# Polysketch attention with a GELU layer on one core: chunk 0 alone first, and chunk 1 on the path of the later chunks

## The chip, the cores and the metric

The kernel runs on one core of one Trainium2 chip. Its time is the device time of one execution in microseconds (us): 259.19 us as the median of three runs (259.06 to 259.92). All matrices are float32. The two weight matrices and the two sketch matrices arrive as float64 and are turned into float32 on the chip.

## The reference

Attention with a product of two sketches as feature map, then an exact GELU layer. Batch 4, 4 heads, 1088 tokens, head size 32, sketch size 8; the layer goes from 128 to 2048 and back to 128.

```python
def phi(x):                                   # S1, S2: 8 x 32
    a = einsum('rd,bhsd->bhsr', S1, x)
    b = einsum('rd,bhsd->bhsr', S2, x)
    return einsum('bhsi,bhsj->bhsij', a, b).reshape(*x.shape[:-1], 64)
q_p, k_p = phi(q), phi(k)
kv  = einsum('bhsf,bhsd->bhfd', k_p, v)       # 64 x 32 for each head
z   = sum(k_p, axis=2)
num = einsum('bhsf,bhfd->bhsd', q_p, kv)
den = einsum('bhsf,bhf->bhs', q_p, z)[..., None] + 1e-6
x   = (num / den).transpose(0, 2, 1, 3).reshape(4352, 128)
h   = x @ w_in                                # 128 -> 2048
g   = 0.5 * h * (1 + erf(h / sqrt(2)))
out = g @ w_out                               # 2048 -> 128
```

## The kernel before

**Chunks and steps.** Each batch has 1088 tokens: two chunks of 512 and a rest of 64. Chunks are numbered n = 0 to 7 (two for each of the four batches), and the four rests together are chunk 8. For a chunk the 2048 hidden channels are taken in 16 slices of 128, called fi = 0 to 15. A step (n, fi) is: `hidden(n, fi)`, the 128x512 product of a slice of w_in with the chunk's attention output `xT[n]` (L721), followed by the GELU on ScalarE (L728). Below, h(n, fi) is that product and p(n, fi) the product of the GELU's result with the slice of w_out.

**Two ways to the output.** `project(n, fi)` (L858) is the plain way: one 128x512 product for each fi, added up in one PSUM bank. `two_products` (L807) is the other: four fi form a block, and seven pairs of half-size products take the place of the four plain ones (a Strassen-like scheme with 7 products in place of 8). It needs sums of the GELU's results, `token_sums` (L772 to L775, four GpSimd operations of 128x512 for a block), and sums of parts of w_out, `channel_sums(i)` (L759 to L762, four GpSimd operations for each piece of w_out). Before the change, chunks 0 and 1 use the plain way for fi 0 to 7 (`USUAL = 8`) and blocks for fi 8 to 15; later chunks use blocks from fi 0 (`first_block`).

**Two ways to the features of the queries.** Chunks 0 and 1 of the first batch use `query_turn` (for chunk 1 four TensorE transposes), `expand_products` with `expand_copy` and `expand_multiply`, then `numerators_by_token`, `divide` and a transpose back (`turn_half` for chunk 1). Later chunks use `query_turn` as one block transpose on VectorE (L528), `query_sketch(n)` (L578), `query_outer(n)`, a run of eleven VectorE lines from L590 to L613, and `attend(n)` (L633, copied to xT at L644). The second way needs the sums of the first batch in another layout: `spread_sketches` (eight GpSimd operations, L477 to L487), `repeat_first_z` (ScalarE copies and one GpSimd copy) and `turn_first_kv` (TensorE, then three small VectorE operations). For chunks 2 and later only batch 1 and above is needed at first, so here `turn_first_kv` comes late, in step 42.

**Rounding of the weights.** w_in and w_out come in five pieces each: pieces 0 and 1 hold two fi, pieces 2, 3 and 4 hold four fi. A piece lands as pairs of 32-bit words, and the class `Rounding` makes float32 of it: `low_words` (ScalarE L260), `fields` (VectorE L268 and L273), `exponents` (ScalarE L279), `mantissas` (VectorE L287, or, with `by_pool`, ScalarE L284 and then GpSimd L285), `signs` (VectorE L292) and `product` (L297, VectorE or GpSimd). h(n, fi) can start only when the piece of w_in is through, p(n, fi) only when that of w_out is.

**Order.** Every engine runs its instructions in the order of the program text (the last loop of the kernel adds this as a dependence). `at(t, f)` puts f into slot t; in step t the loop emits first `hidden`, then `token_sums` at the end of a block, then the slot's functions, then products of earlier steps. The steps of chunks 0 and 1 are interleaved by four fi:

```python
    steps = [(n, fi) for f in range(0, USUAL, 4) for n in range(NCH) for fi in range(f, f + 4)]
    steps += [(n, fi) for n in range(NCHUNK) for fi in range(USUAL if n < NCH else 0, NF)]
```

so that the order is chunk 0 fi 0 to 3, chunk 1 fi 0 to 3, chunk 0 fi 4 to 7, chunk 1 fi 4 to 7, then chunk 0 fi 8 to 15, chunk 1 fi 8 to 15, chunk 2 fi 0 to 15 and so on. Chunk 2 begins in step 32. Every load goes through SP's queue in the order of the text (k and q and v of the first batch, w_in pieces 0 and 1 with q of chunk 1 between them; then, behind a small GpSimd memset that waits for the rounding of w_in piece 0, w_out and w_in pieces 0 to 4, then the other batches).

Of the kernel before, what the change touches and what calls it, by code (L numbers as in the profile page):

```python
# [16 lines left out]
def kernel(  # L17
# [97 lines left out]
    def load_q(n):  # L115
        at = n % NCH * CW
        if n < NCH:
            sp.dma_start(out=q_sb[n], in_=q[0, :, at:at + CW, :].rearrange("h (p j) d -> p h j d", j=JC))  # L118
            return
        for h in range(H):  # L120
            sp.dma_start(out=q_sb[n][h * 32:(h + 1) * 32].rearrange("t x j d -> t (x j d)"),
                         in_=q[n // NCH, h, at:at + CW, :].rearrange("(t n) d -> t (n d)", t=32))
# [75 lines left out]
    load_w_in(0)  # L198
    load_q(1)
    load_w_in(1)  # L200

    def load_rest():

        load_w_out(1, gated=True)
        for i in range(2, len(pieces)):
            load_w_in(i)
            load_w_out(i)
        for b in range(1, B):
            load_keys(b)
            load_values(b)  # L210
            for c in range(NCH):
                load_q(b * NCH + c)
            if b == 1:
                for n, b1 in (("k", 1), ("k", 3), ("v", 1), ("v", 2), ("v", 3)):
                    load_rem(n, b1)
        load_q_rem()
# [26 lines left out]
    class Rounding:  # L243
# [37 lines left out]
        def mantissas(self, by_pool=False):  # L281
            if self.wide and by_pool:
                high = mlp.tile([128, LC // 2], FP, name="bits_high")[:, :self.m.shape[1]]
                act.activation(out=high, in_=self.a, func=ACT.Copy, scale=2.0 ** -20)  # L284
                pool.tensor_add(out=self.m, in0=high, in1=self.low)  # L285
            elif self.wide:
                dve.scalar_tensor_tensor(out=self.m, in0=self.a, scalar=2.0 ** -20, in1=self.low, op0=AX.mult,  # L287
                                         op1=AX.add)
# [209 lines left out]
    def repeat_first_z():  # L498
# [3 lines left out]
        for c in range(NP):  # L502
            act.copy(out=to[:F, c], in_=of[c * F:(c + 1) * F, :, 0:D])
        zs = att.tile([128, 2, D], FP, name="z_cols")
# [15 lines left out]
    def query_turn(n, copy=by_act):  # L520


        if n == 1:
            turned = transposed(work_bank(), "qT", [q_sb[1][:, h].rearrange("p j d -> p (j d)") for h in range(H)], copy)
            qT[n] = turned.rearrange("p (h j t) -> p h j t", h=H, j=JC)
            return
        qT[n] = att.tile([128, H, width[n] // 128, D], FP, name="qT" if n < NMAIN else "qT_rem")
# [184 lines left out]

    first_banks, begun = {}, [(0, 0), (1, 0)]

    def hidden(n, fi, by_halves=False):
# [3 lines left out]
        for rows in (slice(0, 64), slice(64, 128)) if by_halves else (slice(0, 128),):  # L719
            if (n, fi) not in begun:  # L720
                pe.matmul(ps[rows, :W], lhsT=w[:, rows], rhs=xT[n][:, :W], start=True, stop=True)  # L721
        if n < NCH and fi < USUAL:
            g_of[n, fi] = mlp.tile([128, CW], FP, name="g", bufs=4)
        else:
            if fi % NB == 0:
                blocks[n, fi // NB] = block(FP)
            g_of[n, fi] = blocks[n, fi // NB][:, fi % NB]
        act.activation(out=g_of[n, fi][:, :W], in_=ps[:, :W], func=ACT.Gelu)  # L728

    def first_hidden(n, half):  # L730

        if half == 0:
            first_banks[n, 0] = hidden_bank()
        parts = 1 if n else 2
        for i in range(parts):
            cols = slice(half * 256 + i * 256 // parts, half * 256 + (i + 1) * 256 // parts)
            pe.matmul(first_banks[n, 0][:, cols], lhsT=w_tile(w_in_sb, 0), rhs=xT[n][:, cols], start=True, stop=True)  # L737
# [53 lines left out]
    def first_block(n):  # L791
        return USUAL // NB if n < NCH else 0

# [53 lines left out]
    def project(n, fi, parts=range(B // 2), cols=slice(None)):  # L847
        first, final = fi == 0, fi == (USUAL if n < NCH else NF) - 1
        if first:
# [10 lines left out]
    def store(n):  # L860
# [9 lines left out]
        row = n // NCH * S + n % NCH * CW  # L870
        if n < NCH:

            for c in range(d_model // 32):
                to = out[row:row + CW, c * 32:(c + 1) * 32].rearrange("(g t j) d -> j t g d", t=32, j=JC)
                o = oT[c * 32:(c + 1) * 32].rearrange("p n (m d) -> p (n m) d", d=32)
                o = o.rearrange("p (g j) d -> j p g d" if n == 0 else "p (j g) d -> j p g d", j=JC)
                for j in range(JC):
# [48 lines left out]
    w_in[0].exponents()  # L926
    late = []
    query_turn(1, lambda **a: late.append(a))
    kz_of, kv_of = (x.rearrange("f (r x) -> f r x", r=2)[:, :, :C] for x in (kz[0], kv_bank[:, :128]))
    act.copy(out=kz_of, in_=kv_of)  # L930
    w_in[1].fields()
    w_in[0].mantissas()
# [4 lines left out]
    w_out = [Rounding(w, beside=b) for w, b in zip(w_out_sb[:2], w_in)]  # L937
    by_act(**late[0])
    w_in[1].low_words()
    parts = [range(2), range(2, JC)]  # L940
    nd = [[hidden_bank(), hidden_bank()], [out_bank(), out_bank()]]
# [3 lines left out]
    w_in[1].exponents()  # L945
    expand_products(1)
    for banks, tokens, by in zip(nd, parts, (None, den)):
# [3 lines left out]
    for half in range(2):  # L951
        first_hidden(0, half)
    expand_copy(1, 0)
    w_in[1].mantissas()
    w_in[1].signs()
    w_in[1].product()
    expand_copy(1, 1)
    for i in range(2):
        expand_multiply(1, i)
    w_out[0].fields()  # L960


    steps = [(n, fi) for f in range(0, USUAL, 4) for n in range(NCH) for fi in range(f, f + 4)]
    steps += [(n, fi) for n in range(NCHUNK) for fi in range(USUAL if n < NCH else 0, NF)]
    slots = {t: [] for t in range(len(steps) + LAG)}
# [83 lines left out]
    def kv_and_attend(b, n):  # L1049

        banks = held["kv"] = work_banks()
        kv_sum(b, banks[:, 1, CW // 2:])
        if n >= NCH:
            attend(n, banks)
        take_kv(b, banks[:, 1, CW // 2:])

    def round_at(t, w, product_by=dve):
        r = []
        at(t, lambda: (r.append(Rounding(w)), r[0].low_words(), r[0].fields()))
        at(t + 1, lambda: (r[0].exponents(), r[0].mantissas(), r[0].signs(), r[0].product(product_by)))  # L1060

    for i, (t0, t1) in enumerate(((4, 6), (8, 10))):
        round_at(t0, w_in_sb[i + 2])
        round_at(t1, w_out_sb[i + 2])
    round_at(12, w_in_sb[4], pool)
    at(13, channel_sums, 3)

    at(12, widen_v_rem, 1)
    for r in range(2):
        at(14, key_turn_blocks, 1, r)  # L1070
    round_at(14, w_out_sb[4], pool)
    at(15, query_turn, 2)
    at(16, features_of_all, 1)
    at(16, outer_of_all, 1)
    at(16, turn_keys_rem, 1)
    at(17, features_rem, 1)
    at(17, add_tokens, 1)
    at(18, channel_sums, 4)

    at(24, z_sum, 1)  # L1080
    at(24, fold_z, 1)
    at(23, query_turn, 3)
    at(24, kv_and_attend, 1, 1)
    at(24, query_sketch, 2)
    at(26, lambda: turn_kv(1, held["kv"]))
    at(24, query_outer, 2)
    for i, t in enumerate((25, 26, 28)):
        at(t, channel_sums, i)
    at(11, spread_sketches)
    at(40, repeat_first_z)  # L1090
    for n in range(3, NCHUNK):

# [32 lines left out]
        if keys:  # L1125
            at(t + 5 + (n == NCH + 1), outer_of_all, b)
            at(t + 5 + (n == NCH + 1), add_tokens, b)
            at(t + 8, widen_v_rem, b)
            if b == 2:
                at(t + 10, turn_first_kv)  # L1130

# [4 lines left out]
    for t, (n, fi) in enumerate(steps):  # L1136
        if n < NCH and fi < USUAL:
            products[t + LAG].append((project, n, fi))
            if fi == USUAL - 1:
                slots[t + LAG + 1 + 2 * n].append(lambda n=n: take_usual(n))  # L1140
        elif n == NMAIN:
# [8 lines left out]
        elif fi % NB == NB - 1:  # L1150
            b = fi // NB
            opens = b == first_block(n)
            late = int(n < NCH or n == NCH and opens)
            for later, pairs in ((3, 3), (4, 2), (5, 2)) if opens else ((2, 2), (3, 2), (4, 1), (5, 2)):
# [8 lines left out]
    for t in range(len(steps) + LAG):  # L1163
        if t < 4:
# [7 lines left out]
            if t == 2:  # L1172
                w_out[1].low_words()
            if t == 3:
                banks = work_banks()
                numerators_by_token(1, halves(banks), range(JC))
                w_out[1].mantissas(by_pool=True)
                w_out[1].exponents()
                divide(1, banks, range(JC), by_head_pair=False)
                w_out[1].signs()  # L1180
                w_out[1].product()
                project(0, 0)
                project(0, 1, cols=slice(0, 256))
                turn_half(1, 0, work_bank(), by_act)
                project(0, 1, cols=slice(256, 512))
                turn_half(1, 1, work_bank(), by_dve)
            continue
        if t == 4:
            first_hidden(1, 0)
            for f, *a in products[t]:  # L1190
                f(*a)
            first_hidden(1, 1)
        for n in drains[t]:
# [5 lines left out]
        if t < len(steps):  # L1199
            n, fi = steps[t]  # L1200
            hidden(n, fi, by_halves=t >= 18 and (n < NMAIN or fi < 5))
        if t < len(steps) and steps[t][0] < NMAIN and steps[t][1] % NB == NB - 1:
# [5 lines left out]
        for n in done[t]:  # L1208
            store(n)
        if t != 4 and not sooner:  # L1210
            for f, *a in products[t]:
# [42 lines left out]
```

## Time and profile before

| What | Value |
|---|---|
| median of three runs | 259.19 us (259.06 to 259.92) |
| span of the profiled execution | 257.9 us, so about 1.3 us of the median lie around it |
| PE busy | 253.1 us, 98% of the span |
| DVE, ACT, POOL busy | 151.1, 115.2, 163.6 us |
| granted TensorE clock | 0.999 of full |
| h(n, fi), one 128x512 product | 0.86 us from start to start |
| a block pair of `two_products` | 0.43 us |
| starts of h(0, 0), h(0, 8), h(2, 0) in the chain that ended last | 15.31, 45.70, 71.33 us |

PE is TensorE, DVE VectorE, ACT ScalarE, POOL GpSimd, SP the queue that issues loads and stores. In a line of the timeline the first number is the start in us, the second the duration in us, then engine, line of the kernel, operation, tiles and count; in square brackets is the idle time just before and what ended it. A float32 product is two PE instructions, so "x2" is one product. The displayed durations of PE run into each other by some 0.15 us, so that distances between starts are the price.

### The profile page before, as it was taken

The page shows a single profiled execution, that of the slowest core. Times are in us where ns is not written, and L with a number is a line of the kernel's source. Part 1 is how long each engine was busy: PE and PEld are TensorE (multiplying, and loading weights), DVE is VectorE, ACT ScalarE, POOL GpSimd, SP SyncE. Part 2 cuts the span into 40 slices and gives each one's busy share as a digit, 9 for nine tenths or more (in the row PEclk, how much of TensorE's full clock was granted, in tenths as well). Part 3 has the DMA queues.
Part 4 walks back from the last instruction along what each step waited for, and adds up shares of the span by engine and source line. Part 5 has one row for each costly group of instructions (what it writes and reads, how often), then busy time and mean ns, then how long its engine had stood idle before and what let it go on. Part 6 is the DMA issues. An engine that isn't in the chain of part 4 may idle for free.

```text
span 257.9 us, 5770 instructions
## 1 busy us (share of the span) xinstructions
PE 253.1 (98%) x2335; PEld 135.5 (53%) x2335; DVE 151.1 (59%) x313; ACT 115.2 (45%) x224; POOL 163.6 (63%) x173
## 2 busy tenths in 40 slices
PE   8989999999999999999999999999999999999995
PEld 7846444354444545444444455455544444445794
DVE  3786888969699997590178986399307000700330
ACT  4665777433626332543335332533444334433442
POOL 3313006799968778587758775787758777877300
PEclk9999999999999999999999999999999999999999
DMA  6459747751000101102000002000200200020020
GB/s 203 143 156 375 181 117 174 211 131 15 4 0 13 29 3 23 20 8 35 3 0 3 0 10 37 0 1 3 41 3 5 38 0 1 7 36 0 3 41 20
DMA packets 29594, 13.48 MB, mean 52 GB/s; under 512 B 21888, under 2 KB 27776, under 8 KB 29568
## 3 DMA queue, kind: packets, MB, share of 16 engines
q1 hardware_dynamic: 29392, 13.05, 20.2%
q8 instruction: 18, 0.29, 0.5%
q10 hardware_dynamic: 176, 0.07, 0.1%
q14 instruction: 8, 0.07, 0.1%
HBM read 10.88 MB, written 2.23 MB: 51 GB/s over the span
## 4 chain that ended last, share of the span: by engine, by line
PE 93%; SPq 2%; DMA 2%; DVE 1%; issue 0%; ACT 0%
PE h_ps L721 45%; PE o_ps L807 33%; PE o_ps L858 5%; PE w_ps L855 3%; DMA small<-in_moe_w_in_dram 2%; PE w_ps L437 1%; PE w_ps L578 1%; PE w_ps L633 1%; SPq L132 1%; PE h_ps L737 1%; SPq L100 1%; PE w_ps L977 1%; PE w_ps L656 0%; SPq L118 0%; PE w_ps L467 0%
## 5 line engine op out<-in xcount | busy, mean ns | idle before, releaser
L721 PE MATMUL h_ps<-xT,w_in 128*64 128x512 f32 (+3 forms) x514 | 136.9, 576 | 0.0
L728 ACT ACTIVATE block<-h_ps 128x512 f32<-128x512 f32 (+1 forms) x128 | 73.1, 571 | 117.2 <-PE h_ps L721 115.3
L721 PEld LDWEIGHTS h_ps<-xT,w_in 128*64 128x64 f32 (+1 forms) x514 | 41.9, 142 | 30.5 <-issue 11.6
L807 PE MATMUL o_ps<-block,w_out 128*64 128x256 f32 x224 | 57.5, 379 | 0.0
L772 POOL TENSOR_TENSOR bits_low<-block 128x512 f32<-128x512 f32 x28 | 36.0, 1286 | 27.7 <-ACT block L728 27.7
L807 PEld LDWEIGHTS o_ps<-block,w_out 128*64 128x64 f32 x224 | 30.5, 137 | 38.0 <-issue 27.5
L773 POOL TENSOR_TENSOR bits_a<-block 128x512 f32<-128x512 f32 x28 | 35.8, 1278 | 11.8 <-ACT block L728 11.8
L822 DVE COPY sums<-o_ps 64x256 f32<-64x256 f32 x8 | 3.3, 417 | 60.6 <-PE o_ps L807 60.6
L774 POOL TENSOR_TENSOR bits_e<-bits_a,block 128x512 f32<-128x512 f32 x28 | 36.1, 1288 | 2.2
L775 POOL TENSOR_TENSOR bits_m<-block,bits_e 128x512 f32<-128x512 f32 x28 | 35.9, 1282 | 2.2
L807 PE MATMUL o_ps<-bits_a,small 128*64 128x256 f32 x112 | 28.8, 379 | 0.0
L807 PE MATMUL o_ps<-bits_low,small 128*64 128x256 f32 x112 | 28.8, 379 | 0.0
L807 PE MATMUL o_ps<-block,small 128*64 128x256 f32 x112 | 28.8, 379 | 0.0
L807 PE MATMUL o_ps<-bits_m,w_out 128*64 128x256 f32 x112 | 28.7, 379 | 0.0
L807 PEld LDWEIGHTS o_ps<-block,small 128*64 128x64 f32 x112 | 15.2, 137 | 17.9 <-issue 10.8
L807 PE MATMUL o_ps<-bits_e,small 128*64 128x256 f32 x112 | 17.0, 383 | 0.0
L858 PE MATMUL o_ps<-g,w_out 128*128 128x512 f32 (+1 forms) x34 | 16.5, 572 | 0.0
L807 PEld LDWEIGHTS o_ps<-bits_m,w_out 128*64 128x64 f32 x112 | 15.3, 137 | 0.0
L807 PEld LDWEIGHTS o_ps<-bits_a,small 128*64 128x64 f32 x112 | 15.2, 137 | 0.0
L807 PEld LDWEIGHTS o_ps<-bits_low,small 128*64 128x64 f32 x112 | 15.2, 137 | 0.0
L590 DVE STREAM_TRANSPOSE w_ps<-w_ps 128x512 f32<-128x512 f32 (+1 forms) x7 | 4.8, 687 | 17.1 <-ACT xT L644 12.7
L807 PEld LDWEIGHTS o_ps<-bits_e,small 128*64 128x64 f32 x112 | 7.7, 137 | 10.6 <-issue 8.8
(195 smaller groups left out, 303.7 us busy)
## 6 DMA issues: line engine op xcount, KB each, us to landing
block<-in_moe_w_in_dram SPq DMA_DIRECT2D x3, 512.0 KB, 11.3
block<-in_moe_w_out_dram SPq DMA_DIRECT2D x3, 512.0 KB, 14.7
k<-in_k_dram SPq DMA_DIRECT2D x12, 128.0 KB, 2.9
v<-in_v_dram SPq DMA_DIRECT2D x12, 128.0 KB, 3.5
q<-in_q_dram SPq DMA_DIRECT2D x24, 64.0 KB, 2.1
out_dram<-oT SPq DMA_DIRECT2D x21, 64.0 KB, 2.2
k<-in_k_dram SPq DMA_DIRECT2D x2, 256.0 KB, 2.8
q<-in_q_dram SPq DMA_DIRECT2D x2, 256.0 KB, 3.9
```

Of the source, the lines that this page charges most:

```text
L100: eng.dma_start(out=main[n, b][:, heads], in_=src_of[n][b, heads, 0:MAIN, :].rearrange("h (p j) d -> p h j d", j=J))
L590: dve.transpose(out=tok, in_=ps[:, :, :H2])
L721: pe.matmul(ps[rows, :W], lhsT=w[:, rows], rhs=xT[n][:, :W], start=True, stop=True)
L728: act.activation(out=g_of[n, fi][:, :W], in_=ps[:, :W], func=ACT.Gelu)
L772: pool.tensor_sub(out=s[3], in0=a11, in1=a21)
L773: pool.tensor_add(out=s[1], in0=a21, in1=a22)
L774: pool.tensor_sub(out=s[2], in0=s[1], in1=a11)
L775: pool.tensor_sub(out=s[4], in0=a12, in1=s[2])
L807: pe.matmul(acc[n][bank][half * 64:(half + 1) * 64, col:col + HW], lhsT=fixed, rhs=moving, start=opens and e == 0 and name in "4715", stop ...
L822: dve.tensor_copy(out=N[lo, 0, one], in_=a0[lo, one])
L855: pe.matmul(o_of[n][i][:, :128], lhsT=g[:, i * 128:(i + 1) * 128], rhs=w_tile(w_out_sb, fi), start=first, stop=final)
L858: pe.matmul(o_of[n][:, cols], lhsT=w_tile(w_out_sb, fi), rhs=g[:, cols], start=first, stop=final)
```

## The change

Chunk 0 runs through its 16 fi in steps 0 to 15 and chunk 1 through its own in steps 16 to 31. Chunk 0 keeps the old ways; chunk 1 takes the later chunks' way, with `query_turn` on VectorE, `query_sketch(1)`, `query_outer(1)` and `attend(1)`, and with blocks from fi 0. The queries of chunk 1 are loaded after all weights, in the later chunks' layout. `spread_sketches`, `repeat_first_z` and `turn_first_kv` move to steps 4, 5 and 6 (before: 11, 40 and 42). The roundings move too: w_in piece 2 begins in step 2 and ends in step 3, w_out 2 is in step 4, w_in 3 in step 6, w_in 4 in step 8, w_out 3 in step 9, w_out 4 in step 14; in all of them GpSimd does the addition of the mantissas, and in all but w_in 2 the product as well. p(0, 0) to p(0, 3) all stand in step 3.

The diff, cut:

```diff
-        if n < NCH:
+        if n == 0:
             sp.dma_start(out=q_sb[n], in_=q[0, :, at:at + CW, :].rearrange("h (p j) d -> p h j d", j=JC))
...
     load_w_in(0)
-    load_q(1)
     load_w_in(1)
...
             load_w_in(i)
             load_w_out(i)
+        load_q(1)
...
-                high = mlp.tile([128, LC // 2], FP, name="bits_high")[:, :self.m.shape[1]]
+                high = mlp.tile([128, LC], FP, name="bits_high", bufs=1)[:, :self.m.shape[1]]
...
         for c in range(NP):
-            act.copy(out=to[:F, c], in_=of[c * F:(c + 1) * F, :, 0:D])
+            for to_rows in (slice(0, F), slice(F, 2 * F)):
+                act.copy(out=to[to_rows, c], in_=of[c * F:(c + 1) * F, :, 0:D])
...
-        if n < NCH and fi < USUAL:
+        if n == 0 and fi < USUAL:
             g_of[n, fi] = mlp.tile([128, CW], FP, name="g", bufs=4)
...
     def first_block(n):
-        return USUAL // NB if n < NCH else 0
+        return 0 if n else USUAL // NB
...
-    late = []
-    query_turn(1, lambda **a: late.append(a))
...
-    w_in[1].fields()
     w_in[0].mantissas()
...
-    by_act(**late[0])
     w_in[1].low_words()
+    w_in[1].fields()
...
-    expand_products(1)
...
-    expand_copy(1, 0)
...
-    expand_copy(1, 1)
-    for i in range(2):
-        expand_multiply(1, i)
     w_out[0].fields()
-    steps = [(n, fi) for f in range(0, USUAL, 4) for n in range(NCH) for fi in range(f, f + 4)]
-    steps += [(n, fi) for n in range(NCHUNK) for fi in range(USUAL if n < NCH else 0, NF)]
+    steps = [(n, fi) for n in range(NCHUNK) for fi in range(NF)]
...
-    for i, (t0, t1) in enumerate(((4, 6), (8, 10))):
-        round_at(t0, w_in_sb[i + 2])
-        round_at(t1, w_out_sb[i + 2])
-    round_at(12, w_in_sb[4], pool)
-    at(13, channel_sums, 3)
...
+    def round_begin(w):
+        r = Rounding(w)
+        r.low_words()
+        r.fields()
+        r.exponents()
+        return r
+
+    def round_end(r, product_by):
+        r.mantissas(by_pool=True)
+        r.signs()
+        r.product(product_by)
+
+    def round_at(t, w, product_by=pool):
+        at(t, lambda: round_end(round_begin(w), product_by))
+
+    round_at(4, w_out_sb[2])
+    at(4, spread_sketches)
+    at(5, repeat_first_z)
+    round_at(6, w_in_sb[3])
+    at(6, turn_first_kv)
+    at(6, query_turn, 1)
+    at(8, query_sketch, 1)
+    round_at(8, w_in_sb[4])
+    round_at(9, w_out_sb[3])
+    at(9, query_outer, 1)
+    at(10, channel_sums, 3)
     for r in range(2):
-        at(14, key_turn_blocks, 1, r)
-    round_at(14, w_out_sb[4], pool)
-    at(15, query_turn, 2)
-    at(16, features_of_all, 1)
+        at(13, key_turn_blocks, 1, r)
+    at(14, widen_v_rem, 1)
+    round_at(14, w_out_sb[4])
+    at(15, attend, 1)
+    at(15, features_of_all, 1)
...
-    at(18, channel_sums, 4)
...
-    for i, t in enumerate((25, 26, 28)):
+    at(16, channel_sums, 4)
+    for i, t in enumerate((17, 18, 19)):
         at(t, channel_sums, i)
-    at(11, spread_sketches)
-    at(40, repeat_first_z)
...
-            if b == 2:
-                at(t + 10, turn_first_kv)
...
-        if n < NCH and fi < USUAL:
-            products[t + LAG].append((project, n, fi))
+        if n == 0 and fi < USUAL:
+            products[t + LAG if fi >= 4 else 3].append((project, n, fi))
...
             if t == 2:
                 w_out[1].low_words()
-            if t == 3:
-                banks = work_banks()
-                numerators_by_token(1, halves(banks), range(JC))
+                w_out[1].exponents()
                 w_out[1].mantissas(by_pool=True)
-                w_out[1].exponents()
-                divide(1, banks, range(JC), by_head_pair=False)
                 w_out[1].signs()
                 w_out[1].product()
-                project(0, 0)
-                project(0, 1, cols=slice(0, 256))
-                turn_half(1, 0, work_bank(), by_act)
-                project(0, 1, cols=slice(256, 512))
-                turn_half(1, 1, work_bank(), by_dve)
+                third = round_begin(w_in_sb[2])
+            if t == 3:
+                round_end(third, dve)
+                for f, *a in products[t]:
+                    f(*a)
             continue
-        if t == 4:
-            first_hidden(1, 0)
-            for f, *a in products[t]:
-                f(*a)
-            first_hidden(1, 1)
...
-            hidden(n, fi, by_halves=t >= 18 and (n < NMAIN or fi < 5))
+            hidden(n, fi, by_halves=t >= 10 and (n < NMAIN or fi < 5))
```

## The prediction

> **What bounds the kernel now.** I read the page first: busy times, and the chain that ended last.
>
> ```profile
> PE 253.1 (98%) x2335; PEld 135.5 (53%) x2335; DVE 151.1 (59%) x313; ACT 115.2 (45%) x224; POOL 163.6 (63%) x173
> ...
> PE 93%; SPq 2%; DMA 2%; DVE 1%; issue 0%; ACT 0%
> ```
>
> TensorE sets the end and hardly stops. Then the timeline of PE, for what it does while the weights arrive.
>
> ```profile
> 0.77 3.22 PE L890 MATMUL w_ps<-const-float32-0.0 128*128 128x256 f32 x8 [0.77 <-PEq L1238]
> ...
> 29.23 1.02 PE L721 MATMUL h_ps<-xT,w_in 128*128 128x512 f32 x2
> 30.09 1.02 PE L858 MATMUL o_ps<-g,w_out 128*128 128x512 f32 x2
> 30.95 1.02 PE L721 MATMUL h_ps<-xT,w_in 128*128 128x512 f32 x2
> ...
> 45.53 1.02 PE L721 MATMUL h_ps<-xT,w_in 128*128 128x512 f32 x2
> ```
>
> From 24 to 43 us a hidden product and a plain projection alternate without a gap, 0.86 us each. h(0, 4) starts at 29.23 and h(0, 8) at 45.53: the two chunks share the work, so w_in 3 is wanted 16.3 us after w_in 2. Now VectorE, GpSimd, ScalarE and the loads, for how fast pieces can be rounded.
>
> ```profile
> 11.98 0.29 DVE L268 TENSOR_SCALAR bits_e<-small 128x256 uint32<-128x256 uint32 x1 [1.22 <-DMA small<-in_moe_w_in_dram]
> ...
> 13.07 0.22 DVE L673 TENSOR_SCALAR den_tok<-h_ps 128x4 f32<-128x4 f32 x2
> ...
> 27.35 0.69 DVE L297 TENSOR_TENSOR w_in<-bits_m,bits_e 128x512 f32<-128x512 f32 x1
> ...
> 33.97 0.69 DVE L297 TENSOR_TENSOR w_in<-bits_m,bits_e 128x512 f32<-128x512 f32 x1
> ```
>
> ```profile
> 22.47 0.58 POOL L487 COPY S_abc<-S_abc 128x64 f32<-128x64 f32 x3
> ...
> 40.89 1.28 POOL L297 TENSOR_TENSOR w_in<-bits_m,bits_e 128x512 f32<-128x512 f32 x1 [0.77 <-DVE bits_e L292]
> ...
> 49.37 1.28 POOL L772 TENSOR_TENSOR bits_low<-block 128x512 f32<-128x512 f32 x1 [1.15 <-ACT block L728]
> ```
>
> ```profile
> 24.84 0.66 ACT L260 ACTIVATE bits_low<-block 128x512 f32<-128x512 uint32 x1
> 25.40 0.59 ACT L728 ACTIVATE g<-h_ps 128x512 f32<-128x512 f32 x1
> 25.87 0.72 ACT L279 ACTIVATE bits_r<-bits_e,below 128x512 uint32<-128x512 uint32 x1
> ```
>
> ```profile
> 14.01 0.88 SPq L181 DMA_DIRECT2D small<-in_moe_w_out_dram  x2
> ...
> 18.53 4.49 SPq L106 DMA_DIRECT2D k<-in_k_dram  x4
> 25.46 7.04 SPq L113 DMA_DIRECT2D v<-in_v_dram  x4
> ```
>
> VectorE has w_in 3 ready at 34.66, eleven us early. GpSimd pays 1.28 us for a 128x512 operation where VectorE pays 0.69. The loads of v at 25.46 wait for the transfers of w_in 3 to w_out 4, the last by 32.1.
>
> **What goes from TensorE.** Four transposes of q (0.59, from 10.86 to 11.45), 16 products of `expand_products` (1.1), numerators (1.07), transposes back (0.44). Eight plain projections (8 x 0.86 = 6.88) become two blocks of seven pairs (14 x 0.43 = 6.02): 0.86 less. Added: sketch (0.60, 56.64 to 57.24) and attend (0.43), about 1.0. Behind the first hidden product this is 1.07 + 0.44 + 0.86 - 1.0 = 1.4 us less. `turn_first_kv` (0.3) only moves forward across step 32. The other removed products lie in the head, among waits.
>
> **The head.** VectorE no longer waits at 11.98 for w_in 1 before it rounds w_in 0; with 256 KB of q gone from the queue (about 1 us at the 269 GB/s of those slices) w_in 1 also lands near 11.0. den_tok moves from 13.07 to 11.95: all is 1.12 us earlier, so h(0, 0) starts at 15.31 - 1.12 = 14.19, and the gated loads at 12.35 for 14.01. Without the earlier landing it would be 0.67.
>
> **The price: the roundings.** Chunk 0 alone wants pieces twice as fast, and they now pass ScalarE, VectorE and GpSimd behind work that waits for TensorE. I lay the new order of each engine out by rows of before. ScalarE at 128x512: low words 0.66, exponents 0.71, GELU 0.60, the mantissa copy (seen at 128x256 only, 0.42) taken as 0.67; the next starts 0.1 before an end. VectorE: field 0.42, signs or product 0.69. GpSimd: 1.28 each. A handover costs 0.05.
>
> 1. h(0, 3) ends at 17.73. VectorE ends w_out 0 at 18.3 and w_out 1, with GpSimd's addition, at 20.65, and takes the fields of w_in 2 at 20.55 (landed by 22.8 before; 1.65 earlier now, at most 21.2). ScalarE: exponents to 21.73, then g(0, 3), mantissa copy to 22.8; GpSimd adds to 24.1; VectorE's product ends at 24.84. h(0, 4) starts at 24.9. Meanwhile TensorE has only p(0, 0) to p(0, 3), which wait for w_out 0 and 1 and for g(0, 3). Gaps: 0.6 + 0.6 + 0.7 + 1.8 = 3.7.
> 2. g(0, 4) ends at 26.4; behind it on ScalarE stands all of w_out 2 (26.3 to 28.14). GpSimd adds and multiplies to 30.8; behind this stand eight operations of `spread_sketches` (21.32 to 23.05 before, 1.7) and the z copy (about 0.3): 32.75. `turn_first_kv` stands on TensorE after h(0, 6), which ends at 27.5, and ahead of p(0, 4). Gap: 5.3.
> 3. GpSimd's w_in 3 ends at 35.3; h(0, 8) starts at 35.66 without a wait. g(0, 8) ends at 37.2, behind it w_in 4 on ScalarE to 38.94, GpSimd to 41.55; h(0, 12) at 41.75. Gap 0.45. h(0, 15) ends at 45.35.
> 4. w_out 3: VectorE's signs end at 41.35, and only then comes `query_outer(1)`, 57.40 to 63.7 before, 6.35 long: 47.7. `attend(1)` waits for it (gap 2.4); the features of batch 1's keys wait for VectorE's key transposes (49.05, gap 0.85). xT(1) stands on ScalarE behind w_out 4, whose fields VectorE takes at 49.0: 51.7. h(1, 0) starts at 51.75 after a gap of 0.85.
> 5. GpSimd: w_out 3 to 44.15, channel sums 3 (46.40 to 48.22 before) 1.85, token sums (0, 2) 5.2, v's rest 0.5, w_out 4 2.6, token sums (0, 3) 5.2, channel sums 4 1.85: 61.35. The first pair of block (0, 3) needs both, and TensorE arrives there at 56.4. Gap: 5.0.
>
> From there GpSimd (5.2 a block) keeps up with TensorE (4 x 0.86 + 3.01 = 6.45). From 61.4 to h(2, 0): 13 hidden products 11.2, 26 pairs 11.2, the batch's key sums and sketches 1.9 + 0.22 + 1.46: about 87.3, with two more pairs done than before (0.86) and `turn_first_kv` (0.3). Against 71.33 that is 87.3 - 71.33 - 1.16 = 14.8 us later. Check by gaps: 18.6 new, 1.3 of small ones in before's same stretch taken off, 1.4 of work and 1.12 of head off: 14.8. On the time this gives 259.2 + 14.8 = 274.0; the 1.3 around the span stay.
>
> **What a gap does to TensorE's clock.** The trace of before has no long gap but the one ahead of the first product; there 1664 columns of warming products took 3.22 us, which at the later 0.86 for 1024 columns take 1.40. So a gap costs between 0 and 1.8 us behind it. Two of mine exceed 5 us or come to it: 0 to 3.6. I take 1.8, one of two, since the nearest row is the start itself but its idle time is not that of a gap.
>
> The Trainium skill, "TensorE: Matmul & The Clock Gate", Part 1, says that the array falls to half its clock after an idle window of about 3.4 us, and comes back after about as long a busy one; the 656 ns of the first 128x256 products against 379 later agree with half a clock at the start, but no run here shows it in mid-kernel. By this rule each of the two gaps, longer than one window but shorter than two, may or may not hold a whole one; with both, an estimate from that page's 3.4 us is 1.7 us of loss each.
>
> Sum: 274.0 + 1.8 = 275.8.
>
> **What is hidden.** The queries of chunk 1 queue behind all weights, so land near 31; VectorE reaches them at 34.0. SP's later loads shift by four issues of 0.42; keys of batch 1 are wanted at 47.7. The doubled z copies, four of about 0.2 on ScalarE, are in step 2's chain beside GpSimd and cost nothing.
>
> **Bounds.** The channel sums at 42 to 45 took 0.64 to 0.91 instead of 0.46 beside busy VectorE: up to 1.6 more. Small gaps as before: 1.3. With both gaps cold, 274.0 + 3.6 + 1.6 + 1.3 = 280.5, and 1.2 if q lands as late as the slowest keys did (13.8 us after issue at 21.4): 282.
>
> **Rivals.** First: GpSimd's own work alone binds, the waits of step 2 to 4 vanish into it. From 22.85 its operations up to channel sums 4 are 1.28 + 10 x 1.28 + 1.7 + 0.3 + 1.85 + 5.2 + 0.5 + 5.2 + 1.85 = 30.6, ending at 53.45, 8 us earlier than 61.4: 266. For it: the scheme needs only ScalarE to run ahead; against it: ScalarE's roundings stand behind GELUs which wait for TensorE. Second: the loads last. If q_1 lands after 36, each us is one of delay at the sketch: 277 to 279. Against: the rows above give 31. Third, faster: the roundings stay ahead of TensorE, and the 1.4 of work, 0.3 of moved work and 1.1 of head remain: 259.2 - 2.8 = 256.4. It needs all gaps together under 2.8 us; step 1 alone has 3.7. That the change does not do what it says is excluded: the new order of instructions shows blocks of chunk 1 from fi 0.
>
> **Chances.** The chain 0.80 (274 to 282), GpSimd alone 0.12 (266), late loads 0.04, faster 0.04. Range 266 to 282, likeliest 275.8. A measurement of this kernel tells some 0.3% (0.8 us) from no change: faster 0.04, within 0.01, slower 0.95.
>
> **What would show it.** Right: PE gaps of about 5 us before L513 (released by POOL) and before the first L803 of block (0, 3) (by POOL), one before L630 (by DVE), h(2, 0) near 87 to 89. Wrong: no wait at L513, or h(0, 4) before 22, or gaps released by DMA.

## The result, and the profile after

The changed kernel takes 283.5 us (median of four runs, 282.21 to 284.49) against 259.36 us: 1.092 of before (95% interval 1.088 to 1.095), 24.1 us slower. The forecast of 275.8 had the sign and most of the mechanism, but the time lies 1.5 us above its range. The profiled execution took 284.49 us, its span 282.7.

The page after, for the two lines of before that were read first (busy time, and the chain that ended last by engine):

```profile
PE 259.4 (92%) x2315; PEld 134.3 (48%) x2315; DVE 152.6 (54%) x309; ACT 117.1 (41%) x228; POOL 184.7 (65%) x190
...
PE 77%; SPq 8%; POOL 6%; DMA 4%; DVE 2%; issue 1%; ACT 0%; POOLq 0%; DVEq 0%
```

TensorE's share fell from 98% to 92%: it is idle for 23.3 us of the span, 4.8 before. The chain's 8% of SPq and 4% of DMA come in at one GpSimd operation, the channel sum that starts at 51.48; GpSimd was at work until 51.51 (51.06 and 0.45), so the loads held up nothing there. The timeline of PE shows where; its brackets hold the gap and what ended it:

```profile
26.30 2.94 PE L718 MATMUL h_ps<-xT,w_in 128*128 128x512 f32 x6 [1.46 <-DVE w_in L297]
34.82 0.48 PE L513 MATMUL w_ps<-ident,z_cols 128*64 128x64 f32 x4 [5.59 <-POOL z_cols L506]
35.24 2.08 PE L854 MATMUL o_ps<-g,w_out 128*128 128x512 f32 x2
37.10 1.91 PE L718 MATMUL h_ps<-xT,w_in 128*128 128x512 f32 x2
38.81 1.92 PE L854 MATMUL o_ps<-g,w_out 128*128 128x512 f32 x2
40.52 1.27 PE L718 MATMUL h_ps<-xT,w_in 128*128 128x512 f32 x2
...
48.51 3.74 PE L718 MATMUL h_ps<-xT,w_in 128*64 128x512 f32 x16 [1.49 <-ACT block L725]
54.13 0.67 PE L630 MATMUL w_ps<-q_pT,kz_first 64*32 64x256 f32 x16 [1.89 <-DVE q_pT L610]
59.71 1.08 PE L718 MATMUL h_ps<-xT,w_in 128*64 128x512 f32 x4 [2.31 <-ACT xT L641]
68.37 0.69 PE L803 MATMUL o_ps<-block,small 128*64 128x256 f32 x1 [3.22 <-POOL small L758]
```

From the top: h(0, 4) to h(0, 6), then `turn_first_kv` behind 5.59 us of nothing, p(0, 4), h(0, 7), p(0, 5), h(0, 8), then h(0, 12), `attend(1)`, h(1, 0) and the first pair of block (0, 3). Four of these gaps are the forecast's, with the releasers it named. But the products behind the first one start 1.7 to 1.9 us apart instead of 0.86.

VectorE, where the lines L268 and L273 are `fields`:

```profile
12.56 0.83 DVE L273 TENSOR_SCALAR bits_a<-small 128x256 uint32<-128x256 uint32 x1
13.32 0.22 DVE L670 TENSOR_SCALAR den_tok<-h_ps 128x4 f32<-128x4 f32 x2
...
26.16 0.42 DVE L268 TENSOR_SCALAR bits_e<-block 128x512 uint32<-128x512 uint32 x1
...
29.86 1.50 DVE L268 TENSOR_SCALAR bits_e<-block 128x512 uint32<-128x512 uint32 x1
31.29 1.49 DVE L273 TENSOR_SCALAR bits_a<-block 128x512 uint32<-128x512 uint32 x1
...
36.78 0.83 DVE L268 TENSOR_SCALAR bits_e<-block 128x512 uint32<-128x512 uint32 x1
...
44.22 1.52 DVE L268 TENSOR_SCALAR bits_e<-block 128x512 uint32<-128x512 uint32 x1
45.66 1.50 DVE L273 TENSOR_SCALAR bits_a<-block 128x512 uint32<-128x512 uint32 x1
```

One form (128x512), two durations: 0.42 us, or 1.5, with one of 0.83 between. The timeline of GpSimd at the same moments:

```profile
12.52 0.73 POOL L297 TENSOR_TENSOR w_in<-bits_m,bits_e 128x256 f32<-128x256 f32 x1 [2.46 <-DVE bits_e L292]
...
29.82 1.26 POOL L285 TENSOR_TENSOR bits_m<-bits_high,bits_low 128x512 f32<-128x512 f32 x1 [4.30 <-ACT bits_high L284]
31.16 1.34 POOL L297 TENSOR_TENSOR w_out<-bits_m,bits_e 128x512 f32<-128x512 f32 x1
...
34.54 0.23 POOL L506 COPY z_cols<-kz 128x64 f32<-128x64 f32 x1
...
36.07 1.27 POOL L297 TENSOR_TENSOR w_in<-bits_m,bits_e 128x512 f32<-128x512 f32 x1
...
44.18 1.27 POOL L285 TENSOR_TENSOR bits_m<-bits_high,bits_low 128x512 f32<-128x512 f32 x1 [6.84 <-ACT bits_high L284]
45.53 1.34 POOL L297 TENSOR_TENSOR w_in<-bits_m,bits_e 128x512 f32<-128x512 f32 x1
```

Each 1.5 us field lies over a GpSimd addition or product and ends 0.28 or 0.29 us after it: 31.36 behind 31.08, 32.78 behind 32.50, 45.74 behind 45.45, 47.16 behind 46.87. The field at 36.78 began late in the product of 36.07, which ends at 37.34, and took 0.83. So a slowed field lasts as long as what is left of the GpSimd operation beside it, and then a little. (The 128x256 field at 12.56 lies in the same way over the product at 12.52.) GpSimd itself stands idle for 4.3 and 6.8 us until ScalarE has copied a mantissa, and ScalarE, in its own timeline, waits for those same fields with a GELU queued behind:

```profile
47.25 0.63 ACT L284 ACTIVATE bits_high<-bits_a 128x512 f32<-128x512 uint32 x1 [0.75 <-DVE bits_a L273]
47.78 0.58 ACT L725 ACTIVATE block<-h_ps 128x512 f32<-128x512 f32 x1
```

That GELU is what h(0, 12) at 48.51 waits for.

### The profile page after: what moved, and what is told of

It reads as the page before. It is cut to its first block, busy times and chain, and to the rows that moved or that the text cites. A ratio compares the mean times of both kernels' runs of the same rounds, so it can differ in the third digit from the quotient of the medians.

```text
span 282.7 us, 5739 instructions
## 1 busy us (share of the span) xinstructions
PE 259.4 (92%) x2315; PEld 134.3 (48%) x2315; DVE 152.6 (54%) x309; ACT 117.1 (41%) x228; POOL 184.7 (65%) x190
## 4 chain that ended last, share of the span: by engine, by line
PE 77%; SPq 8%; POOL 6%; DMA 4%; DVE 2%; issue 1%; ACT 0%; POOLq 0%; DVEq 0%
PE h_ps L718 36%; PE o_ps L803 32%; DMA block<-in_moe_w_out_dram 3%; PE w_ps L851 3%; SPq L121 2%; SPq L113 2%; SPq L106 1%; PE w_ps L437 1%; PE w_ps L886 1%; PE w_ps L575 1%; PE w_ps L630 1%; SPq L132 1%; DMA q<-in_q_dram 1%; POOL bits_m L771 1%; POOL bits_e L770 1%
## 5 line engine op out<-in xcount | busy, mean ns | idle before, releaser
L718 PE MATMUL h_ps<-xT,w_in 128*64 128x512 f32 (+3 forms) x532 | 139.7, 582 | 5.3 <-ACT xT L641 2.3
L725 ACT ACTIVATE block<-h_ps 128x512 f32<-128x512 f32 (+1 forms) x136 | 77.8, 572 | 130.3 <-PE h_ps L718 128.4
L803 PE MATMUL o_ps<-block,w_out 128*64 128x256 f32 x240 | 61.8, 380 | 0.0
L768 POOL TENSOR_TENSOR bits_low<-block 128x512 f32<-128x512 f32 x30 | 38.6, 1287 | 28.8 <-ACT block L725 28.8
L803 PEld LDWEIGHTS o_ps<-block,w_out 128*64 128x64 f32 x240 | 32.7, 137 | 40.6 <-issue 29.3
L769 POOL TENSOR_TENSOR bits_a<-block 128x512 f32<-128x512 f32 x30 | 38.2, 1272 | 16.0 <-ACT block L725 15.9
L771 POOL TENSOR_TENSOR bits_m<-block,bits_e 128x512 f32<-128x512 f32 x30 | 38.4, 1281 | 2.4
L803 PE MATMUL o_ps<-block,small 128*64 128x256 f32 x120 | 31.8, 388 | 3.2 <-POOL small L758 3.2
L803 PE MATMUL o_ps<-bits_low,small 128*64 128x256 f32 x120 | 31.8, 388 | 0.0
L285 POOL TENSOR_TENSOR bits_m<-bits_high,bits_low 128x512 f32<-128x512 f32 (+1 forms) x7 | 8.3, 1188 | 22.4 <-ACT bits_high L284 22.3
```

The source lines that it names most:

```text
L768: pool.tensor_sub(out=s[3], in0=a11, in1=a21)
L769: pool.tensor_add(out=s[1], in0=a21, in1=a22)
L771: pool.tensor_sub(out=s[4], in0=a12, in1=s[2])
L803: pe.matmul(acc[n][bank][half * 64:(half + 1) * 64, col:col + HW], lhsT=fixed, rhs=moving, start=opens and e == 0 and name in "4715", stop ...
```

## The experiments

Three theories stood at the start. The chain: the roundings pass three engines behind work that waits for TensorE. The clock: what the forecast left out is TensorE at half speed behind the gaps. The contention: what it left out is VectorE made slower by GpSimd. In all kernels but `e5_before_pool` the edit is made to the changed kernel. None leaves work out; `e1_warm`, `e7_dve_busy` and `e9_warm_all` add useless work.

**e1_warm: products of zeros in the longest gap.**

```diff
         ps, zs = work_bank(), held["zs"]
+        keep_busy(12, ps)        # 12 products 128x256 ahead of turn_first_kv
```

> The changed kernel (283.5 us) with twelve products of zeros, 128x256, on TensorE ahead of turn_first_kv, so 5.2 us of work without use in the gap of 5.6. Theory: the four 128x512 products behind that gap ran at 1.7 us instead of 0.86 because TensorE's clock fell in the gap; kept busy, the granted clock stays at 1.0 from 34 to 42 us, L513 still waits for the z copy to about 34.8, and the time falls by about 3.0 to 280.5. Rival: the slow products come from something else beside them (GpSimd and VectorE at work), then the time stays at 283.5.

Measured: 280.87 us, 1.082 [1.076, 1.087]; 2.6 less. The timeline of PE of this run:

```profile
25.67 4.54 PE L719 MATMUL h_ps<-xT,w_in 128*128 128x512 f32 x6 [1.46 <-DVE w_in L297]
30.05 5.39 PE L887 MATMUL w_ps<-const-float32-0.0 128*128 128x256 f32 x24
...
35.63 1.12 PE L855 MATMUL o_ps<-g,w_out 128*128 128x512 f32 x2
36.59 1.02 PE L719 MATMUL h_ps<-xT,w_in 128*128 128x512 f32 x2
```

The products behind the gap are back at 0.86 to 0.96 from start to start, at a granted clock of 1.00: the slow ones were the clock, not their data. (The z copy was through at 34.88, the zeros only at 35.4, so they held `turn_first_kv` back by some 0.5 us.) In this run h(0, 4) to h(0, 6) took 4.54 us instead of 2.94, at a granted clock of 0.58, with no gap over 1.5 us ahead.

**e2_early: the sketches spread before chunk 0.** `spread_sketches` and GpSimd's z copy move ahead of the steps, where GpSimd is idle.

```diff
     load_w_out(0, gated=True)
     load_rest()
+    spread_sketches()
+    repeat_first_z_cols()        # the GpSimd copy out of repeat_first_z
...
-    at(4, spread_sketches)
```

> The changed kernel with spread_sketches and the z copy on GpSimd put into its idle time after the memsets of the head (13 to 21 us), instead of behind the rounding of w_out 2. Theory (order on GpSimd): L513 does not wait any more; the next wait is p(0, 4) for w_out 2, ready at 32.5 where h(0, 6) ends at 29.2, so a gap of 3.3 in place of 5.6: 2.3 less, and up to 3.0 more if the clock holds through the shorter gap: 278 to 281. Rival (the gap is the roundings' alone): the wait only moves to p(0, 4) with its length, 283.5.

Measured: 281.3 us, 1.083 [1.079, 1.088]; 2.2 less, just above the expected 278 to 281. `turn_first_kv` starts at 30.09 without a wait, and the timeline of PE shows what is late next:

```profile
30.09 0.34 PE L516 MATMUL w_ps<-ident,z_cols 128*64 128x64 f32 x4
32.78 2.08 PE L857 MATMUL o_ps<-g,w_out 128*128 128x512 f32 x2 [2.35 <-POOL w_out L297]
```

p(0, 4) now waits for GpSimd's product of w_out 2, and runs at half clock as before. This run too has half clock at h(0, 4) to h(0, 6) (0.61 from 26 to 30 us).

**e3_dve: all roundings from w_in 2 on put on VectorE, all else as changed.** (Before the change GpSimd had the products of w_in 4 and w_out 4; here they are on VectorE as well.)

```diff
-        r.mantissas(by_pool=True)
+        r.mantissas()
...
-    def round_at(t, w, product_by=pool):
+    def round_at(t, w, product_by=dve):
```

> The changed kernel with the additions and products of w_in 2 to w_out 4 on VectorE as before the change (0.69 each instead of 1.28 on GpSimd). Theory: h(0, 4) comes 1.5 us earlier (no handover to GpSimd), w_out 2 is through by 30, spread and z copy run while GpSimd is idle, so the 5.6 gap falls to at most 1.6 and with it the cold clock; VectorE's fields at 128x512 take 0.42 again instead of 1.50, the query part starts earlier, and channel and token sums have no roundings ahead of them: 265 to 270. Rival (the engine does not matter, chunk 0 alone simply wants weights too early): 279 or more.

Measured: 270.96 us, 1.045 [1.043, 1.047]: 12.5 us less, somewhat short of the expected drop. The fields are at 0.42 us again, and `turn_first_kv` follows h(0, 6) at once. PE's list of waits (total, times, longest) shows what is left of the straight order:

```profile
PE w_ps L630 <- DVE q_pT L610: 3.2, 1, 3.2
PE o_ps L854 <- DVE w_out L297: 2.2, 3, 1.2
...
PE o_ps L803 <- POOL small L758: 0.6, 1, 0.6
```

VectorE now does all the rounding, and TensorE reaches `attend(1)` ahead of the end of `query_outer`: it waits 3.2 us, and behind it the granted clock is 0.58 for 4 us.

**e5_before_pool: only the other part, in the kernel before.** The old interleaved order, with GpSimd's addition and product in every `round_at`. (The tile of the copied mantissas is made as wide as in the changed kernel.)

```diff
-    def round_at(t, w, product_by=dve):
+    def round_at(t, w, product_by=pool):
...
-r[0].exponents(), r[0].mantissas(), r[0].signs()
+r[0].exponents(), r[0].mantissas(by_pool=True), r[0].signs()
```

> The kernel before the change (259.3 us), its steps interleaved as they were, but all roundings of w_in 2 to w_out 4 with addition and product on GpSimd as in the changed kernel. Theory: interleaved steps leave w_in 3 eleven us of slack, and each rounding gets only 1.2 us longer, so 259 to 261 us. Rival: GpSimd's roundings by themselves cost the time whatever the order of steps: 270 or more.

Measured: 262.7 us, 1.013 [1.011, 1.015]: more than the expected 259 to 261, far from the rival's 270. Its waits of PE:

```profile
PE o_ps L807 <- POOL bits_e L774: 1.5, 1, 1.5
...
PE h_ps L721 <- POOL w_in L297: 0.5, 1, 0.5
```

The swap of engines costs 3.2 us here and 12.5 in the straight order. The slow fields are here as well (L268 at 27.20 takes 1.51 us, L273 at 28.63 takes 1.49), so it is the order that decides how much of them is seen. Where a piece is wanted every 16 us, a slower rounding is nearly covered; where it is wanted every 8, it is not.

**e6_sooner: w_out 2 rounded a step earlier.**

```diff
             if t == 3:
+                fourth = round_begin(w_out_sb[2])
                 round_end(third, dve)
+                round_end(fourth, pool)
...
-    round_at(4, w_out_sb[2])
```

> The changed kernel (283.5 us) with the rounding of w_out 2 put from step 4 into step 3, so that on ScalarE its three operations stand ahead of g(0, 4), which waits for h(0, 4), and on VectorE its fields ahead of the product of w_in 2. Nothing else is moved, GpSimd does the same work. Theory (the gap at L513 comes from ScalarE's order): GpSimd's addition for w_out 2 starts at 26.2 instead of 29.8, the z copy ends near 31 instead of 34.8, the gap falls from 5.6 to about 2, and less clock is lost: 276 to 280. Rival (GpSimd's throughput sets the pace from here on, so it waits later for what it gains now): 282 or more.

Measured: 280.91 us, 1.083 [1.079, 1.088]; 2.6 less, between the expected 276 to 280 and the rival's 282. From its waits of PE:

```profile
PE h_ps L718 <- DVE w_in L297: 2.7, 1, 2.7
PE h_ps L718 <- ACT xT L641: 2.3, 1, 2.3
PE h_ps L718 <- POOL w_in L297: 2.3, 1, 2.3
...
PE w_ps L513 <- POOL z_cols L506: 0.5, 1, 0.5
```

The 5.6 us gap is 0.5, but h(0, 4) waits 1.2 longer and h(0, 8) waits 2.3 where it had not waited. As in `e2_early`, one gap of the chain can be closed and a good part of it comes back at the next piece: 2.4 of 5.6 us there, 3.5 of 5.1 here.

**e7_dve_busy: contention by itself.** `e3_dve`, with ten GpSimd products of a scratch tile, on which nothing depends, in step 6.

```diff
+    for i in range(10):
+        at(6, lambda: pool.tensor_mul(out=scratch, in0=scratch, in1=scratch))
```

> The run with all roundings on VectorE (270.96 us), with ten two-input GpSimd products of 128x512 on a scratch tile added in step 6, where GpSimd is idle from 24.5 to 39.5; nobody reads them. Theory (VectorE's fields stand still while GpSimd runs such operations): L268 and L273 at 128x512 for w_in 3, w_in 4 and w_out 3 take about 1.5 us instead of 0.42, each of these roundings ends some 2 us later, and the time rises by 2 to 5 us to 273 to 276. Rival (the 1.50 us of the changed kernel came from its own operands or buffers): fields stay at 0.42 and the time at 271.

Measured: 276.99 us, 1.068 [1.064, 1.073]: 6.0 us more than `e3_dve`, and more than the expected 273 to 276. GpSimd's timeline, then VectorE's:

```profile
25.42 13.52 POOL L1067 TENSOR_TENSOR scratch<-scratch 128x512 f32<-128x512 f32 x10
```

```profile
27.77 0.69 DVE L287 SCALAR_TENSOR_TENSOR bits_m<-bits_a,bits_low 128x512 f32<-128x512 uint32 x1 [0.85 <-ACT bits_low L260]
28.38 1.53 DVE L292 SCALAR_TENSOR_TENSOR bits_e<-block,bits_r 128x512 uint32<-128x512 uint32 x1
29.94 1.41 DVE L297 TENSOR_TENSOR w_out<-bits_m,bits_e 128x512 f32<-128x512 f32 x1
31.27 1.26 DVE L268 TENSOR_SCALAR bits_e<-block 128x512 uint32<-128x512 uint32 x1
...
39.69 0.42 DVE L273 TENSOR_SCALAR bits_a<-block 128x512 uint32<-128x512 uint32 x1
```

Eight of the nine 128x512 operations of the roundings that started in those 13.5 us took 1.25 to 1.53 us, whether alone they take 0.42 or 0.69 (one, at 27.77, did not), 6.27 us more in all; GpSimd's ten took 1.35 each, hardly more than the 1.28 it needs anyway. VectorE pays here, and nearly all of it reached the end: `query_outer` starts at 46.37 instead of 39.40, 0.94 of which was there ahead of the scratch products (this profile lost clock in the head), so 6.03 behind them; `attend(1)` waits for it in both runs, and the time is 6.0 longer. GpSimd's own later work is not what moved: its channel sums began at 39.56 in `e3_dve`, and the scratch ended at 38.94.

It is not always VectorE that pays. In `e3_dve` two of GpSimd's token sums, at 48.53 and 50.14, took 1.65 and 1.71 us instead of 1.28 beside two-input operations of VectorE. And not every VectorE operation is slowed: a block transpose of the queries takes 0.71 us beside GpSimd's product in the changed kernel (at 36.15) and 0.71 with GpSimd idle in `e3_dve` (at 32.86).

**e8_best: every repair together.** `e3_dve` with the early sketches of `e2_early`, w_out 2 in step 3 and `attend(1)` later among the products of step 15.

```diff
+                round_end(round_begin(w_out_sb[2]), dve)     # step 3
...
-    at(15, attend, 1)
-    at(15, features_of_all, 1)
+    products[15] += [(attend, 1), (features_of_all, 1)]
```

> Straight order with its waits taken out as far as the runs show them: all roundings on VectorE (270.96), w_out 2 rounded in step 3, spread and z copy in GpSimd's idle time of the head, and attend(1) with the key features moved behind the first three pairs of block (0, 2), so that the query work on VectorE (to 45.8) is covered. Theory: p(0, 4) no longer waits 1.2, the gap of 3.25 at attend falls below 1, and the half clock from 46 to 50 goes: 265 to 267, so still slower than before the change, since h(0, 4) waits for w_in 2 whatever is done behind it. Rival (what is left is the clock or GpSimd): 269 or more. A result under 259 would mean that the straight order itself costs nothing.

Measured: 270.89 us, 1.045 [1.043, 1.047]: no less than `e3_dve`, against an expected 265 to 267; the rival's 269 or more came true. Its waits of PE:

```profile
PE h_ps L721 <- ACT xT L644: 2.6, 1, 2.6
PE o_ps L806 <- POOL bits_e L773: 1.5, 1, 1.5
...
PE h_ps L721 <- DVE z_s L492: 1.1, 1, 1.1
```

`attend(1)` no longer waits, but h(1, 0) waits for xT(1), which stands on ScalarE behind the exponents of w_out 4. These wait for a field at 46.47 that takes 1.64 us beside a GpSimd token sum, and behind the gap of 2.6 the granted clock is 0.65 from 50 to 54 us: contention and clock took back what the moves had gained. Nothing tried in the straight order comes near 259.2.

**e9_warm_all: zeros in five gaps.**

```diff
+        if (n, fi) in ((0, 4), (1, 0)):
+            keep_busy(3 if n == 0 else 5, ps)
...
+            keep_busy(4, banks[:, 0])        # attend(1)
...
+        if t == 18:
+            keep_busy(7, held["rem"])        # block (0, 3)
```

(and the 12 of `e1_warm`.)

> The changed kernel with zero products of 128x256 in five of TensorE's gaps: 3 ahead of h(0, 4), 12 ahead of turn_first_kv, 4 ahead of attend(1), 5 ahead of h(1, 0), 7 ahead of block (0, 3); all fit into the gaps measured. Theory (what was mis-sized is the clock): granted clock 1.0 from 22 to 74 us, all products at 0.86, and the time falls by the 3.0 lost after the first gap and the 1.7 after the second, to about 278.8. Rival (a warm array waits the longer at the next handover): no better than the 280.9 of the run with twelve products alone.

Measured: 280.03 us, 1.080 [1.077, 1.083], between the expected 278.8 and the rival's 280.9. The granted clock (the third figure from the end of a window's line; behind the first comma is PE's busy time) is 1.00 in every window from 18 to 94 us, also where the changed kernel lost it:

```profile
34.00:38.00 4.00, 3.65 (x15) 1.87 (x14) 2.40 (x6) 0.46 (x2) 3.73 (x8) 1.00 0.33 61
...
66.00:70.00 4.00, 4.00 (x30) 2.05 (x30) 0.89 (x2) 0.98 (x2) 3.84 (x10) 1.00 0.00 0
```

So half clock in mid-kernel is worth 3.5 us of the time, and some 20.7 of the 24.1 us have another cause. This profile lost clock in the head (0.57 from 14 to 18 us), so 3.5 may be a little low.

## Where the prediction was right, and where it was wrong

Slower, the chain of waits and its releasers came as forecast; the size did not, by 7.7 us, and the time lies above the range. In the trace after, h(2, 0) came 9.6 us after the forecast's 87.3, and 274.0 + 9.6 = 283.6 is near the measured median (the traced execution itself took 284.49). Behind h(2, 0) the span is 185.8 us, 186.7 before, nearly the 1.16 less of the forecast. So the miss lies ahead of h(2, 0), and can be read step by step (forecast without its 1.8 for the clock):

| Point | forecast | measured | late | new since the point above |
|---|---|---|---|---|
| h(0, 4) | 24.9 | 26.3 | 1.4 | 1.4 |
| `turn_first_kv` | 32.8 | 34.8 | 2.0 | 0.6 |
| h(0, 8) | 35.7 | 40.5 | 4.8 | 2.8 |
| h(0, 12) | 41.75 | 48.5 | 6.8 | 2.0 |
| `attend(1)` | 47.75 | 54.1 | 6.4 | -0.4 |
| h(1, 0) | 51.75 | 59.7 | 8.0 | 1.6 |
| block (0, 3) | 61.4 | 68.4 | 7.0 | -1.0 |
| h(2, 0) | 87.3 | 96.9 | 9.6 | 2.6 |

**"The head": wrong by 1.4 us.** All was to be 1.12 us earlier; in the timeline h(0, 0) begins at 15.39, and at 15.15 before. den_tok started at 13.32 instead of 11.95. Some 0.5 of it is a field that the new order put beside GpSimd's product of w_in 0: 0.83 us instead of 0.29, and 0.83 or 0.84 in every run of the changed order. Most of the rest is the start: the key products took 0.69 and 0.63 us at 5.42 and 5.90 (0.44 and 0.38 before). That differs from execution to execution: in `e9_warm_all`, whose head is the same, they took 0.44 and 0.38, and h(0, 0) began at 14.52, 0.63 earlier than before, so there the field accounts for the rest of the 1.12. Why the start is sometimes slower is open.

**The chain, steps 1 to 5: right in its waits, and in their sum.** The gaps of step 1 were put at 3.7 us and measured 0.51 + 0.49 + 0.45 + 1.46 = 2.9; step 2's at 5.3, measured 5.6; `attend`'s at 2.4, measured 1.9; block (0, 3)'s at 5.0, measured 3.2, because TensorE reached it late itself. Only h(0, 12) (0.45, measured 1.5) and h(1, 0) (0.85, measured 2.3) were well short, both through fields of 1.5 us. All these gaps together were put at 18.6 us and measured 17.4. The 0.6 at `turn_first_kv` is partly GpSimd's own: one of the small sketch operations took 0.69 instead of 0.23 beside VectorE.

The forecast's check by gaps does not hold. It takes off 1.3 us of small gaps in before's stretch from h(0, 0) to h(2, 0), but before's chain runs there, from 15.31 to 71.33, without idle time. Without the 1.3 the check gives 16.1 instead of the chain's 14.8, so their agreement was luck, and the chain had priced TensorE's own work too low: from h(0, 8) to the end of h(0, 11) at 5.6 us, 6.3 at full clock in `e9_warm_all`; from block (0, 3) to h(2, 0) at 25.9, 26.9 in `e3_dve`.

**"What a gap does to TensorE's clock": mis-sized.** The forecast took 1.8 us for one of two gaps. Both lost clock, the shorter one too. The windows of the trace after, in stretches of 4 us:

```profile
34.00:38.00 4.00, 3.18 (x8) 1.51 (x9) 2.43 (x6) 0.00 (x0) 3.26 (x7) 0.52 0.36 70
38.00:42.00 4.00, 4.00 (x21) 1.49 (x20) 0.00 (x0) 0.78 (x2) 0.00 (x0) 0.62 0.82 216
...
66.00:70.00 4.00, 1.63 (x8) 1.00 (x10) 3.36 (x4) 0.00 (x0) 3.84 (x11) 0.79 0.00 0
70.00:74.00 4.00, 4.00 (x24) 1.66 (x22) 0.00 (x0) 0.81 (x2) 3.19 (x5) 0.78 0.00 0
```

About 3.0 us went behind the first (the 2.8 at h(0, 8)) and 1.7 behind the second (within the 2.6 at h(2, 0)); 4.7 locally, 3.5 of it in the time by `e9_warm_all`. That is close to the forecast's own upper bound of 3.6. Shorter gaps are not safe either: in `e6_sooner` the clock was 0.57 from 38 to 42 us behind a gap of 2.28, while the changed kernel's gap of 2.31 ahead of h(1, 0) cost nothing.

The Trainium skill, "TensorE: Matmul & The Clock Gate", Part 1, has half a clock after an idle window of about 3.4 us in a window that runs freely. The runs agree with the half rate and with a varying phase; here a gap of 3.2 us was enough, and `e1_warm` and `e2_early` fell to it at 26 us behind gaps of at most 1.5 us and a TensorE that was busy for 5.1 of the 8 us before it, which the stated idle window alone does not give.

**The step that failed most, "The price: the roundings": `fields` at 0.42 us whatever GpSimd does beside it.** The forecast knew of such contention only for GpSimd's channel sums, up to 1.6 us in "Bounds" and none in the sum, and took `fields` at 0.42 and 0.42 in every step. Its own layout put them beside GpSimd's operations. They measured 1.37 to 1.52 in three of the roundings, some 2.1 us more for each pair: at 29.9 hidden, since TensorE came to h(0, 8) late anyway; at 44.2 on the path to the GELU that h(0, 12) waits for (a gap of 1.5 instead of 0.45: 1.0 of the 2.0 there); at 55.2 on the path to xT(1) (a gap of 2.3 instead of 0.85: 1.5 of the 1.6). With the 0.5 of the head that is some 3.0 us of the miss, read from the trace after. No run takes the contention alone out of the changed kernel; `e7_dve_busy` shows the cause by itself in another.

The Trainium skill, "GPSIMD Engine Reference", Specifications, says that GpSimd shares its SBUF interfaces with VectorE, and that VectorE's instructions with two SBUF inputs or in its 2-port modes contend. `e7_dve_busy` agrees for the two-input rows (0.69 to 1.34 and more), and the one-input field is slowed too (0.42 to 1.26); whether it runs in such a mode no run here shows.

**The sum.** Of the 9.6 us beyond 274.0, for which the forecast had taken 1.8: clock 4.7, contention 3.0, the rest of the head 0.9. The 1.0 left is small terms of both signs: 0.6 at `turn_first_kv`, 1.7 of TensorE's own work, and the two points that came nearer to the forecast (-0.4 and -1.0).

**The rivals.** GpSimd alone (266) is out: it stood idle 4.30 and 6.84 us for ScalarE, as the argument against it said. Late loads are out: no wait of TensorE in the trace after is released by a DMA. Faster is out in every version of the straight order.

**What the 24.1 us are.** The change with its roundings on VectorE costs 11.5 (`e3_dve`), the move of the roundings to GpSimd another 12.5; how the 12.5 divide between GpSimd's longer operations, the handovers, the contention and the clock no run separates. Nor does any run part the straight order from chunk 1's other path: of `e3_dve`'s waits, 3.9 us (for `q_pT`, `z_s` and `qT`) and the half clock behind `attend(1)` belong to that path.

For the 11.5: the span of `e3_dve` is 11.2 us longer than before's; its waits of PE, without the first at the start of the program, are 8.1 us more than before's, the half clock behind `attend(1)` some 1.3 (from `attend(1)` to the last pair 3.96 us, 2.66 in `e6_sooner`), and by the forecast 1.4 of work is saved. About 3.2 us are left. Most of them may lie at the gaps: products that stand between gaps take 1.10 and 1.13 us instead of 0.86, two take 1.98 instead of 1.72, three 2.94 instead of 2.58, and this 0.24 to 0.36 is not in the idle time of the brackets. An estimate from these rows for `e3_dve`'s eight gaps behind h(0, 0) is 1.9 to 2.9 us.

## What to carry to other kernels

Interleaving two chunks doubled the time between two deadlines of the weight pieces; a straight order needs the same roundings in half of it, and the work saved (1.4 us by the forecast) is small against that. When a plan moves element-wise work to GpSimd, look at what VectorE does beside it: in these traces a field or a two-input operation of VectorE, 0.42 or 0.69 us alone, lasted until the GpSimd operation beside it was through, and a little beyond. So price each such operation at GpSimd's length, not only GpSimd's at its own. And price a gap of TensorE with the slow products behind it: 5.6 and 3.2 us cost 3.0 and 1.7 here, and 2.3 us lost clock in one run and none in another.

## What the runs showed of the hardware that was not expected

In the changed kernel and in `e7_dve_busy` a VectorE field of 128x512 took 0.42 us alone and 1.25 to 1.52 beside a GpSimd operation with two inputs, a two-input operation 0.69 and 1.34 to 1.53, while GpSimd's went from 1.28 to only 1.35. The slowed fields of the changed kernel ended 0.27 to 0.29 us after the GpSimd operation beside them, also the one that had started late in it. Behind a gap of 5.6 us TensorE gave a product in 1.7 us instead of 0.86 for some 6 us of work, and a gap of 3.2 us cost 1.7 us. The clock fell behind different gaps in different kernels: at 26 us in `e1_warm` and `e2_early`, at 34 in the changed kernel, though the work ahead was alike.
